# A fused attention and two-MLP kernel: later units with two heads swapped, exponentials with sums on ScalarE, one rectifier, and one block's weights split on chip

## The chip, the cores and the metric

The kernel runs on one core of a Trainium2 chip. The metric is the device time of one execution in microseconds (us), the median over runs. The engines that matter are TensorE (PE, matrix products; PEld are its weight loads), VectorE (DVE), ScalarE (ACT) and SyncE (SP), from whose queue nearly all DMAs are issued. GpSimd (POOL) only sets up constants.

## The reference

q, k and v are [8 batches, 8 heads, 576 positions, 64]. The MLP weights come as 64-bit floats. What is computed:

```python
# attention within chunks of 64 positions
scores = scale * q_c @ k_c.T            # 9 chunks of 64x64 for each batch and head
scores -= max(scores); attn = exp(scores); attn /= sum(attn) + 1e-9
x = attn @ v_c                          # heads side by side: x is [4608, 512]
# first MLP, 2048 hidden features
h = x @ w_in
x = (max(h, 0) + alpha * min(h, 0)) @ w_out
# second MLP, 1536 hidden features
g = x @ w_gate
out = (g * sigmoid(g) * (x @ w_val)) @ w_out2
```

## The kernel before

**Blocks.** The 4608 tokens are nine blocks of 512. Blocks 0 to 7 are the first 512 positions of each batch; block 8, the odd one, is the last 64 positions of all eight batches. Activations stand with features on the partitions and tokens along the free dimension.

**Products.** Each float32 operand is split into two float32r parts, a rounded high one (a copy, on ACT or DVE) and the remainder (a subtraction, DVE). `mm3` (L532) makes one product of three PE instructions of 128x512 columns. Blocks go through an MLP in pairs by a Strassen-like scheme with seven products in place of eight (`operands`, `layer1`, `layer2`). Blocks 0, 1 and 8 of the first MLP and block 0 of the second go singly and plainly (`plain1`, `plain2`): for each of 16 tiles of hidden features, `plain1` takes a weight tile from the function `weights(m)`, does twelve instructions into bank Y0 or Y1 and hands the bank to `outs`. While blocks 0 and 1 go through, the 64-bit weights are converted to float32 (`convert`, `new_tile`), split (`whole`), and stored in DRAM: the split parts of each block of the weight matrix in a `Layer` (`lay_in`, `lay_out`, `lay_b`, `lay_out2`), and the first layer's float32 tile `c` in `cd` (L812). `cs` is a ring of three such tiles, `wring` one of seven split tiles, `hring` (h) one of two.

**Block 8's first layer** (L921) takes `weights = stored(lay_in, ...)` (L678): two loads of 256 KB for each of 16 tiles, each load a split quarter with both of its parts, straight into a tile of `wring`.

**Attention** (L384). A unit is one block and one pair of heads, so there are 36. The heads of a pair, j = 0 and 1, stand on partitions 0 to 63 and 64 to 127. The 16 units of blocks 0 to 3 are `early`: they transpose q and k on PE (L430) through banks X0 and X1 and have the scores in W0 and W1. The 20 later units (blocks 8, 4, 5, 6, 7, started at given products by `heads`, L871) run inside the MLP of other blocks, transpose q and k on DVE, and use banks a0 and a1 alone. For the softmax DVE takes the maximum (L452) and subtracts it (L454) for each head, ACT does one exponential of the whole tile `pp` (L457), DVE sums (L458), inverts (L460) and multiplies (L464). PE transposes the probabilities into a0 (L468), a copy makes `pT`, and the product with v (L472 to L477) goes into a1: for each of eight chunks, head 0 from partitions 0 to 63 to 0 to 63 and head 1 from 64 to 127 to 64 to 127. Each of these float32 products is two PE instructions of 64x64. The result goes through `xo` to x1d in DRAM, or for the first eight units (`direct`) straight into operands.

**The rectifier** (`leaky`, L689): from the sum h (or straight from the bank, where `s` is None) ACT makes max(h, 0) and max(-h, 0) (L705, L706), the second into a tile of `hring`, and DVE joins them with -alpha (L714). Another form, on DVE alone (L710), stands as an alternative and does not appear in the trace.

**The order.** All work is put as items into `Program` with its engine, a cost in us, the items that it depends on, and a latency. `order` (L50) simulates these costs, gives each item a due time that it derives backwards from the chained PE products (`main=True`), and writes out one static order; copies may go to ACT or to DVE, whichever the simulation finds better. Each engine, and SP's queue, then works through its own instructions in that order. Until the first product PE gets filler matmuls (L974).

## Time and profile before

| | |
|---|---|
| median of 3 runs | 1733.77 us (1724.03 to 1735.01) |
| the profiled execution | 1724.21 us, of it 1722.4 from the first to the last instruction |
| PE busy | 1644.0 us (95% of the span) |
| DVE busy | 1232.2 us (72%) |
| ACT busy | 915.0 us (53%) |
| first product of the first layer starts | at 46.67 us |
| block 8's first layer, second layer | from 450.20 us, from 507.30 us |

PE is busy nearly all the time, DVE and ACT are not, and their work lies beside PE's. What one of them does costs time only where PE waits for it. Since queues are static, an instruction that waits holds up all that stands behind it on its engine.

### The profile page before, as it was taken

The page shows a single profiled execution, that of the slowest core. Times are in us where ns is not written, and L with a number is a line of the kernel's source. Part 1 is how long each engine was busy: PE and PEld are TensorE (multiplying, and loading weights), DVE is VectorE, ACT ScalarE, POOL GpSimd, SP SyncE. Part 2 cuts the span into 40 slices and gives each one's busy share as a digit, 9 for nine tenths or more (in the row PEclk, how much of TensorE's full clock was granted, in tenths as well). Part 3 has the DMA queues.
Part 4 walks back from the last instruction along what each step waited for, and adds up shares of the span by engine and source line. Part 5 has one row for each costly group of instructions (what it writes and reads, how often), then busy time and mean ns, then how long its engine had stood idle before and what let it go on. Part 6 is the DMA issues. An engine that isn't in the chain of part 4 may idle for free.

```text
span 1722.4 us, 26328 instructions
## 1 busy us (share of the span) xinstructions
PE 1644.0 (95%) x9260; PEld 1336.3 (78%) x9260; DVE 1232.2 (72%) x2188; ACT 915.0 (53%) x1614; POOL 1.0 (0%) x8
## 2 busy tenths in 40 slices
PE   6999998999989799999999999999999999999998
PEld 5777886778767687877788788778778888788877
DVE  5787886898667689877666964688769534774475
ACT  5777646774453677554444633564576432543352
POOL 0000000000000000000000000000000000000000
PEclk9999999999999899999999999999999999999999
DMA  8978878778999995788755597897855855576555
GB/s 191 264 255 247 291 254 277 236 224 234 247 262 322 324 352 191 264 275 290 273 194 194 187 237 228 215 258 226 258 190 186 283 201 191 190 218 210 195 185 146
DMA packets 350835, 407.57 MB, mean 237 GB/s; under 512 B 208624, under 2 KB 229104, under 8 KB 350704
## 3 DMA queue, kind: packets, MB, share of 16 engines
q1 hardware_dynamic: 348640, 405.89, 75.1%
q8 instruction: 73, 1.20, 0.3%
q14 instruction: 58, 0.48, 0.1%
q10 hardware_dynamic: 2064, 0.01, 0.1%
HBM read 307.24 MB, written 98.57 MB: 236 GB/s over the span
## 4 chain that ended last, share of the span: by engine, by line
PE 52%; DMA 2%; DVE 2%; ACT 1%; issue 0%; DVEq 0%; SPq 0%; ACTq 0%
PE X L533 9%; PE X L534 9%; PE X L535 9%; PE W L533 5%; PE W L535 5%; PE W L534 5%; PE Y L534 2%; PE Y L535 2%; PE Y L533 2%; PE X L672 1%; DMA raw<-in_moe_w_gate_dram 1%; PE W L672 1%; DMA raw<-in_moe_w_val_dram 1%; PE a L476 1%; DVE h L237 0%
## 5 line engine op out<-in xcount | busy, mean ns | idle before, releaser
L533 PE MATMUL X<-op,w 128*128 128x512 f32 x1024 | 407.5, 398 | 22.0 <-DVE h L237 12.3
L534 PE MATMUL X<-op,w 128*128 128x512 f32 x1024 | 401.3, 392 | 0.0
L535 PE MATMUL X<-op,w 128*128 128x512 f32 x1024 | 401.1, 392 | 0.0
L533 PEld LDWEIGHTS X<-op,w 128*128 128x128 f32 x1024 | 193.4, 189 | 75.9 <-ACT s L232 19.1
L232 ACT ACTIVATE op<-g 128x512 fp32r<-128x512 f32 x300 | 182.3, 629 | 125.4 <-PE X L534 44.4
L533 PE MATMUL Y<-op,w 128*128 128x512 f32 x560 | 223.5, 399 | 4.4 <-ACT g L743 2.4
L535 PEld LDWEIGHTS X<-op,w 128*128 128x128 f32 x1024 | 193.6, 189 | 40.8
L534 PEld LDWEIGHTS X<-op,w 128*128 128x128 f32 x1024 | 193.5, 189 | 38.2
L533 PE MATMUL W<-op,w 128*128 128x512 f32 x544 | 213.7, 393 | 9.0 <-ACT h L232 8.9
L534 PE MATMUL Y<-op,w 128*128 128x512 f32 x560 | 219.0, 391 | 1.3 <-DVE w L237 1.3
L535 PE MATMUL Y<-op,w 128*128 128x512 f32 x560 | 218.9, 391 | 0.0
L237 DVE TENSOR_TENSOR op<-g,op 128x512 fp32r<-128x512 f32 x300 | 195.6, 685 | 27.5 <-ACT op L232 22.9
L535 PE MATMUL W<-op,w 128*128 128x512 f32 x544 | 212.3, 390 | 0.0
L534 PE MATMUL W<-op,w 128*128 128x512 f32 x544 | 212.2, 390 | 0.0
L232 ACT ACTIVATE s<-X 128x512 f32<-128x512 f32 x172 | 102.4, 597 | 111.0 <-PE X L535 109.6
L237 DVE TENSOR_TENSOR h<-Y,s 128x512 f32<-128x512 f32 x86 | 58.9, 689 | 142.7 <-PE Y L535 141.7
L533 PEld LDWEIGHTS Y<-op,w 128*128 128x128 f32 x560 | 105.7, 189 | 29.1 <-ACT g L743 2.9
L533 PEld LDWEIGHTS W<-op,w 128*128 128x128 f32 x544 | 102.4, 188 | 31.7 <-ACT h L232 9.7
L534 PEld LDWEIGHTS Y<-op,w 128*128 128x128 f32 x560 | 105.7, 189 | 23.1 <-DVE w L237 2.3
L535 PEld LDWEIGHTS Y<-op,w 128*128 128x128 f32 x560 | 105.5, 188 | 22.5
L535 PEld LDWEIGHTS W<-op,w 128*128 128x128 f32 x544 | 102.4, 188 | 21.4
L534 PEld LDWEIGHTS W<-op,w 128*128 128x128 f32 x544 | 102.5, 188 | 21.0
(146 smaller groups left out, 2096.2 us busy)
## 6 DMA issues: line engine op xcount, KB each, us to landing
w<-l_out SPq DMA_DIRECT2D x168, 512.0 KB, 3.7
w<-l_b SPq DMA_DIRECT2D x126, 512.0 KB, 4.3
w<-l_in SPq DMA_DIRECT2D x56, 512.0 KB, 5.0
l_b<-w SPq DMA_DIRECT2D x84, 256.0 KB, 3.3
l_out<-cw SPq DMA_DIRECT2D x80, 256.0 KB, 4.7
l_in<-w SPq DMA_DIRECT2D x64, 256.0 KB, 4.1
raw<-in_moe_w_out_dram SPq DMA_DIRECT2D x28, 512.0 KB, 5.1
w<-l_in SPq DMA_DIRECT2D x56, 256.0 KB, 4.9
```

Source lines behind the costliest of these rows:

```text
L232: pr.add([("ACT", act(n), lambda: na.activation(out=dst, in_=src, func=AF.Copy), False), ("DVE", dvep(n) if psum else dve1(n), lambda: nv. ...
L237: item("DVE", dve2(n), lambda: nv.tensor_tensor(out=dst, in0=a, in1=b, op=op), reads, writes, **kw)
L476: npe.matmul(out=bank["a1"][rs, ts], lhsT=v4[rs, c, :], rhs=pT[rs, ts], start=True, stop=True)
L533: npe.matmul(out=acc, lhsT=w[:, 0, wk], rhs=x[:, 0, :n], start=first, stop=False, skip_group_check=True)
L534: npe.matmul(out=acc, lhsT=w[:, 1, wk], rhs=x[:, 0, :n], start=False, stop=False, skip_group_check=True)
L535: npe.matmul(out=acc, lhsT=w[:, 0, wk], rhs=x[:, 1, :n], start=False, stop=stop, skip_group_check=True)
L672: npe.matmul(out=acc, lhsT=t[:, gp, a * P:(a + 1) * P], rhs=w[:, :, wp, :], start=first and i == 0, stop=stop and i == 2, skip_group_check ...
```

## The change

- Block 8's first layer gets `weights = split_again`: one load of 256 KB of the float32 tile from `cd` into a tile of `cs`, and a split on chip by `whole` (a copy and a subtraction). The parts that only `stored` read from there (number 21, eight of them) are no longer stored in `lay_in`.
- In all units the subtractions and the sum on DVE go. DVE scales the two maxima by -scale (eight columns); ACT then does eight exponentials of 128x64, for each head's bank one for each pair of chunks, straight from the bank into `pp`, with the scaled maximum as bias and the sum as second output.
- In later units (`turn`) the chunks are numbered so that each transposed tile of `pp` holds, for the second half of the chunks, the heads swapped: head 1 on partitions 0 to 63 and head 0 on 64 to 127. V is loaded to match, in four DMAs instead of two. The product with v then goes from partitions j to partitions j into a1 for the first half and crosswise into a0 for the second, the four kinds in turn. `xo` is copied in two halves.
- The rectifier is h + (1 - alpha) max(-h, 0): one rectification on ACT, one joining step on DVE, which now reads h itself; no tile of `hring` where `s` is None. The cost given to the planner for ACT is halved.

```diff
-    lay_in = Layer("l_in", uses1(qa) + [(x, 21) for x in qa])
+    lay_in = Layer("l_in", uses1(qa))
...
+        turn = not early
...
+                for c0, n, r in ((0, 4, j), (4, 4, 1 - j)) if turn else ((0, NCH, j),):
+                    src = v[i, 2 * hp + j, c0 * CH:(c0 + n) * CH, :].rearrange("(c p) e -> p c e", p=CH) \
+                        if i < B else v[c0:c0 + n, 2 * hp + j, NB:S, :].rearrange("b p e -> p b e")
+                    nsp.dma_start(out=v4[r * 64:(r + 1) * 64, c0:c0 + n], in_=src)
...
+        def chunk(cc, c2):
+            return NCH // 2 * (cc % 2) + cc // 2 * 2 + c2 if turn else 2 * cc + c2
...
-            item("DVE", 0.43, partial(nv.tensor_tensor, out=p4[:, :, j, :], in0=sc[j],
-                                      in1=mx[:, j].to_broadcast([P, NCH // 2, CH]), op=ALU.subtract),
-                 [mk], ["pp", sb_[j]])
-        item("ACT", 0.63, lambda: na.activation(out=pp, in_=pp, func=AF.Exp, scale=scale), [], ["pp"])
-        item("DVE", 0.62, lambda: nv.tensor_reduce(out=sm, in_=p4, axis=AX.X, op=ALU.add), ["pp"], [sk])
+        item("DVE", 0.17, partial(nv.tensor_scalar, out=mx, in0=mx, scalar1=-scale, scalar2=None, op0=ALU.mult),
+             [], [mk])
+        def exps(j):
+            for cc in range(NCH // 2):
+                h = j ^ (turn and cc % 2)
+                na.activation(out=p4[:, cc, h, :], in_=sc[j][:, cc, :], func=AF.Exp, scale=scale, bias=mx[:, j, cc],
+                              accum_out=sm[:, cc, h])
+        for j in range(2):
+            item("ACT", 0.96, partial(exps, j), [mk], ["pp", sk, sb_[j]])
...
-            for c in range(NCH):
-                for j in range(2):
-                    rs, ts = slice(64 * j, 64 * j + 64), slice(CH * c, CH * c + CH)
-                    npe.matmul(out=bank["a1"][rs, ts], lhsT=v4[rs, c, :], rhs=pT[rs, ts], start=True, stop=True)
-        item("PE", 1.2, pv, ["pT", kv], ["a1"])
+            for x in range(NCH // 2):
+                for y, j in ((0, 0), (0, 1), (1, 0), (1, 1)):
+                    cc, c2, r = 2 * (x // 2) + y, x % 2, j ^ (turn and y)
+                    c, rs = chunk(cc, c2), slice(64 * r, 64 * r + 64)
+                    npe.matmul(out=bank["a0" if turn and y else "a1"][64 * j:64 * j + 64, CH * c:CH * c + CH],
+                               lhsT=v4[rs, c, :], rhs=pT[rs, (2 * cc + c2) * CH:(2 * cc + c2 + 1) * CH],
+                               start=True, stop=True)
+        pb = ["a1", "a0"] if turn else ["a1"]
+        item("PE", 0.75 if turn else 1.2, pv, ["pT", kv], pb)
...
-        copy_(xo, bank["a1"], NB, [], [xk, "a1"])
+        for y, b in enumerate(pb):
+            h = slice(y * G, (y + 1) * G) if turn else slice(0, NB)
+            copy_(xo[:, h], bank[b][:, h], NB // len(pb), [], [xk, b])
...
-        def relus():
-            how["relu"] = True
-            na.activation(out=g, in_=src, func=AF.Relu)
-            na.activation(out=h, in_=src, func=AF.Relu, scale=-1.0)
+        def minus():
+            how["minus"] = True
+            na.activation(out=g, in_=src, func=AF.Relu, scale=-1.0)
...
-                nv.scalar_tensor_tensor(out=g, in0=h, scalar=nal, in1=g, op0=ALU.mult, op1=ALU.add)
+                nv.scalar_tensor_tensor(out=g, in0=g, scalar=rest, in1=src, op0=ALU.mult, op1=ALU.add)
...
-        pr.add([("ACT", 2 * act(n), relus, False),
-                ("DVE", dvep(n) if psum else dve1(n), lows, not psum)], rd, [gk, tk, *wr])
+        pr.add([("ACT", act(n), minus, False),
+                ("DVE", dvep(n) if psum else dve1(n), lows, not psum)], rd, [gk, *wr])
...
+    def split_again(m):
+        c, ck = cs.next()
+        dma(NB * 4 * P, lambda: nsp.dma_start(out=c, in_=cd[m]), [("cd", m)], [ck])
+        return whole(c, ck)
...
-        plain1(qa, [(x, 0)], partial(stored, lay_in, IN, a_), leak)
+        plain1(qa, [(x, 0)], split_again, leak)
```

## Rows read from the trace of the kernel before

**Rows 1.** The head of the page: span, and busy time of each engine.
```profile
span 1722.4 us, 26328 instructions
PE 1644.0 (95%) x9260; PEld 1336.3 (78%) x9260; DVE 1232.2 (72%) x2188; ACT 915.0 (53%) x1614; POOL 1.0 (0%) x8
```

**Rows 2.** Busy time by stretch: start:end, length, then engines, clock, DMA share, GB/s.
```profile
0.00:47.00 47.00, 31.03 (x462) 26.97 (x463) 24.15 (x55) 26.01 (x35) 0.98 (x8) 0.93 0.83 189
47.00:180.00 133.00, 125.65 (x1176) 101.18 (x1175) 110.00 (x220) 95.61 (x167) 0.00 (x0) 0.99 0.86 260
430.00:490.00 60.00, 55.27 (x414) 44.01 (x413) 41.60 (x79) 27.73 (x52) 0.00 (x0) 1.00 0.96 240
490.00:565.00 75.00, 67.30 (x485) 53.70 (x483) 50.44 (x105) 32.21 (x65) 0.00 (x0) 0.98 0.99 307
1060.00:1200.00 140.00, 138.07 (x1058) 110.58 (x1057) 101.35 (x186) 74.24 (x118) 0.00 (x0) 1.00 0.80 226
```

**Rows 3.** PE's waits, 430 to 600 us: for whom, us in total, times, longest.
```profile
PE W L533 <- ACT h L232: 7.6, 1, 7.6
PE a L468 <- DVE pp L237: 6.8, 4, 3.6
PE a L476 <- ACT pT L232: 4.3, 2, 2.4
PE Y L533 <- ACT h L706: 1.2, 1, 1.2
```

**Rows 4.** PE's timeline around one V product and one group of scores: start, length.
```profile
355.09 1.15 PE L476 MATMUL a<-pT,v 64*64 64x64 f32 x32 [0.69 <-ACT pT L232]
356.17 0.50 PE L533 MATMUL X<-op,w 128*128 128x512 f32 x1
...
364.55 0.69 PE L445 MATMUL a<-kT,qT 64*64 64x64 f32 x32
365.18 0.50 PE L533 MATMUL W<-op,w 128*128 128x512 f32 x1
```

**Rows 5.** The same two, instructions in flight in their first 0.1 us.
```profile
355.09 0.27 PE L476 MATMUL a<-pT,v 64*64 64x64 f32 x2 [0.69 <-ACT pT L232]
...
364.55 0.29 PE L445 MATMUL a<-kT,qT 64*64 64x64 f32 x4
```

**Rows 6.** Groups by line and shape: count, busy us, mean ns; ACT reading banks.
```profile
L232 ACT ACTIVATE s<-W 128x512 f32<-128x512 f32 x86 | 50.9, 593 | 85.2 <-PE W L535 84.6
...
L232 ACT ACTIVATE c<-W 128x256 f32<-128x256 f32 x4 | 1.3, 382 | 3.4 <-DMA out_dram<-c 2.2 <-PE W L672 1.3
```

**Rows 7.** The same view: the softmax steps that go, and a split's subtraction.
```profile
L458 DVE TENSOR_REDUCE sm<-pp 128x8 f32<-128x512 f32 x36 | 24.4, 677 | 19.3 <-ACT pp L457 18.7
L457 ACT ACTIVATE pp<-pp 128x512 f32<-128x512 f32 x36 | 22.8, 632 | 27.5 <-DVE pp L977 27.5
...
L237 DVE TENSOR_TENSOR w<-c,w 128x512 fp32r<-128x512 f32 x32 | 22.0, 687 | 8.5 <-ACT w L232 8.5
...
L977 DVE TENSOR_TENSOR pp<-a,mx 128x256 f32<-128x256 f32 x40 | 17.0, 424 | 1.3
```

**Rows 8.** Busy time by stretch of line 706, the second rectifier, alone.
```profile
47.00:180.00 133.00, 19.15 (x32) 0.99 0.86 260
```

**Rows 9.** PE's waits, 0 to 200 us: the longest in total.
```profile
PE X L430 <- DMA qk<-in_k_dram: 10.2, 9, 2.0
```

**Rows 10.** ACT's timeline in block 8's first layer.
```profile
457.97 0.60 ACT L706 ACTIVATE h<-Y 128x512 f32<-128x512 f32 x1 [3.26 <-DMA x2d<-h]
458.47 0.59 ACT L705 ACTIVATE g<-Y 128x512 f32<-128x512 f32 x1
```

**Rows 11.** DMA issues, 430 to 490 us: count, size, median us to landing.
```profile
w<-l_in SPq DMA_DIRECT2D x32, 256.0 KB, 5.5
```

**Rows 12.** Groups by line and shape: ACT's strided copy of transposed q.
```profile
L232 ACT ACTIVATE qT<-X 128x512 f32<-128x512 f32 x16 | 17.6, 1102 | 8.6 <-PE X L430 8.1 <-PE W L445 0.3
```

More of the change, by code (lines that the diff above doesn't have):

```diff
@@ L195, in attention_moe_moe2 @@
     alpha_sb = one("alpha_sb", [P, KF])
-    nalpha_sb = one("nalpha_sb", [P, KF])
-    zero = one("zero", [P, KF])
+    rest_sb = one("rest_sb", [P, KF])
+    ones = one("ones", [P, KF])
     ops = Ring(sb, "op", 14, [P, 2, NB], F32R)
@@ L417, in load_v @@
             for j in range(2):
-                src = v[i, 2 * hp + j, 0:NB, :].rearrange("(c p) e -> p c e", p=CH) if i < B else \
-                    v[:, 2 * hp + j, NB:S, :].rearrange("b p e -> p b e")
-                nsp.dma_start(out=v4[j * 64:(j + 1) * 64], in_=src)
+                for c0, n, r in ((0, 4, j), (4, 4, 1 - j)) if turn else ((0, NCH, j),):
+                    src = v[i, 2 * hp + j, c0 * CH:(c0 + n) * CH, :].rearrange("(c p) e -> p c e", p=CH) \
+                        if i < B else v[c0:c0 + n, 2 * hp + j, NB:S, :].rearrange("b p e -> p b e")
+                    nsp.dma_start(out=v4[r * 64:(r + 1) * 64, c0:c0 + n], in_=src)
         item("SP", 0.9 if early else 1.9, lambda: load(tq, q), [], [kq], lat=2.2, **gate)
@@ L442, in scores @@
                 for j, c2 in ((0, 0), (1, 1), (0, 1), (1, 0)):
-                    c = 2 * cc + c2
+                    c = chunk(cc, c2)
                     rs, ts = slice(64 * j, 64 * j + 64), slice(CH * c, CH * c + CH)
@@ L692, in leaky @@
         g, gk = gts[j][c][:, :n], ("g", j, c)
-        t, tk = hring.next()
-        h = t[:, :n]
         if s is not None:
-            add2(h, acc, s[0], ALU.add, n, [s[1]], [tk, b], psum=True)
-            src, rd, wr = h, [tk], []
+            t, tk = hring.next()
+            src = t[:, :n]
+            add2(src, acc, s[0], ALU.add, n, [s[1]], [tk, b], psum=True)
+            rd, wr = [tk], []
         else:
             src, rd, wr = acc, [], [b]
-        al, nal = alpha_sb[:, m:m + 1], nalpha_sb[:, m:m + 1]
+        al, rest = alpha_sb[:, m:m + 1], rest_sb[:, m:m + 1]
         how = {}
-        def relus():
-            how["relu"] = True
-            na.activation(out=g, in_=src, func=AF.Relu)
-            na.activation(out=h, in_=src, func=AF.Relu, scale=-1.0)
+        def minus():
+            how["minus"] = True
+            na.activation(out=g, in_=src, func=AF.Relu, scale=-1.0)
         def lows():
-            how["relu"] = False
+            how["minus"] = False
             nv.tensor_scalar(out=g, in0=src, scalar1=0.0, scalar2=al, op0=ALU.min, op1=ALU.mult)
         def join():
-            if how["relu"]:
-                nv.scalar_tensor_tensor(out=g, in0=h, scalar=nal, in1=g, op0=ALU.mult, op1=ALU.add)
+            if how["minus"]:
+                nv.scalar_tensor_tensor(out=g, in0=g, scalar=rest, in1=src, op0=ALU.mult, op1=ALU.add)
             else:
@@ L717, in leaky @@
         psum = s is None
-        pr.add([("ACT", 2 * act(n), relus, False),
-                ("DVE", dvep(n) if psum else dve1(n), lows, not psum)], rd, [gk, tk, *wr])
-        item("DVE", dve2(n), join, rd, [gk, tk, *wr], port=not psum)
+        pr.add([("ACT", act(n), minus, False),
+                ("DVE", dvep(n) if psum else dve1(n), lows, not psum)], rd, [gk, *wr])
+        item("DVE", dve2(n), join, rd, [gk, *wr], port=not psum)
     def to_x2(m, c, acc, b, s, n, pair):
@@ L847, in attention_moe_moe2 @@
         make_identity(nc, ident)
-        ng.memset(zero, 0.0)
+        ng.memset(ones, 1.0)
         na.dma_start(out=alpha_sb, in_=alpha.rearrange("(m p) -> p m", p=P))
-        ng.tensor_tensor(out=nalpha_sb, in0=zero, in1=alpha_sb, op=ALU.subtract)
+        ng.tensor_tensor(out=rest_sb, in0=ones, in1=alpha_sb, op=ALU.subtract)
         leak = partial(leaky, n=NB)
```

## The prediction

> **What bounds the kernel now.** I read the head of the page first: a span of 1722.4 us in a profiled execution of 1724.2, with TensorE (PE) busy 95% of it [rows 1]. Next comes the busy time by stretch [rows 2]. Between 1060 and 1200 us, where eight attention units run inside another layer, PE is busy 138.07 of 140 us. There a microsecond of PE work is a microsecond of time, and one of VectorE (DVE) or ScalarE (ACT) is not. The stretches that differ are the start (PE busy 31.03 of 47 us, part of that filler) and the odd block, block 8: 55.27 of 60 and 67.30 of 75 us, with the DMA share at 0.96 and 0.99 against 0.80 elsewhere. The last view for this is what PE waited for from 430 to 600 us [rows 3]: 6.8 us in four waits for DVE's normalised probabilities, 4.3 us in two for ACT's copy pT, 1.2 us for a rectifier and 7.6 us, once, for ACT's eviction of block 8. So the kernel is PE-bound, with holes in block 8 and at the start that come from late chains. The first kind of saving is PE work anywhere; the second is whatever makes those chains earlier.
>
> **The change part by part.**
>
> *Heads swapped in later units.* Now the product with V takes 32 instructions on two quarters of PE, from 355.09 to the next product at 356.17: 1.08 us. The scores, also 32 instructions of 64x64, use all four quarters and take 364.55 to 365.18: 0.63 us [rows 4]. The first moments tell why: 2 instructions of the former are in flight just after its start, and 4 of the latter [rows 5]. After the change the later units' V product visits the four quarters in turn, as the scores do, so I price it at the scores' 0.63: 0.45 us saved in each of the 36 - 16 = 20 later units, 9.0 us in all. The bounds are 0 and 9.0. Nothing hides this, for it is PE time; only a unit that stands in a hole already may lose it to the wait behind. The probabilities' transposes and the scores keep their number. V's load becomes four issues instead of two with the same bytes; x1's copy becomes two halves, 0.38 + 0.38 us against 0.59 [rows 6], both behind the product, and the plan sets the store 12 us ahead of need.
>
> A rule speaks against this part. In the trace, the V product of before has both of its instructions in flight at once, and these two read partitions 0 to 63 and 64 to 127 and write one bank, a1 [rows 5]. The Trainium skill, "TensorEngine Tiling (Array Packing)", Restrictions and Gotchas, says that different row tiles cannot access the same PSUM bank simultaneously. By that rule the swapped product, which still puts two row tiles into each of a0 and a1, would not reach the scores' rate and its term would be 0 instead of 9.0; the trace disagrees, since the two did run together.
>
> *Exponentials with sums on ScalarE.* DVE loses two subtractions of 0.42 and a sum of 0.68 and gains a tiny scaling, about 0.2: 1.3 us less per unit, 47 us over 36 units. ACT loses one exponential of 0.63 and gains eight of 128x64, each with a bias per partition and a sum [rows 7]. No row shows such an instruction. From ACT's reads of PSUM, 593 ns for 512 columns and 382 for 256 [rows 6], 64 columns extrapolate to 382 - 192 x 0.824 = 224 ns. That is the lower bound (1.8 us a unit), and 382 the upper (3.1). I take 0.30, above the lower because bias and sum come on top: 2.4 us, 1.8 more than now per unit. The skill's page "ScalarE: Activation LUTs", What ACT_TABLE_LOAD costs, gives 280 ns + 0.833 ns a column with a pointer bias and 93 ns of overlap, from which I estimate 240 ns in a row; by it a unit's extra would be 1.3 us instead of 1.8, and no run here shows it yet.
>
> On the path this matters where something waits. The softmax chain itself hardly moves: DVE is 1.3 shorter, ACT 1.8 longer. But four exponentials now stand together on ACT (1.2 us), and copies that free a bank queue behind them. Between 1060 and 1200 us I allow 2 us of new PE waits for that, against the 2 us of holes there now. At the start I allow 2 more: ACT is busy 26.01 of 47 us, so five units' extra (9 us) fits, and from 47 to 180 us the remaining eleven add 20 to 95.61 of 133 while the rectifier takes off 16 (below) [rows 2, 8]. PE's waits at the start are mostly for loads of q and k (10.2 us for k alone, nine waits [rows 9]), which the change leaves alone. Four microseconds together; bounds 0 and 36 (16 early units x (8 x 0.36 - 0.63) if fully exposed).
>
> *One rectifier.* ACT's second rectification goes: about 0.5 us from start to start [rows 10], 32 times before 180 us [rows 8]. DVE's joining step keeps its length but now reads its input itself, so the bank of a direct product stays taken until DVE is through. The buffer h is not used by direct products any more: at 457.97 the second rectifier waited 3.26 us for an earlier store of h [rows 10], and PE 1.2 us for it [rows 3]. That wait goes: 1.2 us. Otherwise ACT is not the bound, so the rest is counted at nothing; if DVE were late with the join, PE would wait for the bank.
>
> *Block 8's first layer from float32 tiles.* Its 32 loads of 256 KB between 430 and 490 us [rows 11] become 16, so 4.2 MB and 16 issues go. At the 307 GB/s of the next stretch [rows 2] that is 13.7 us of transfer out of a stretch whose queues are full. Eight stores of 256 KB at the start go too, at a share of 0.86: counted at nothing. In exchange come 16 splits, 0.63 on ACT (a copy like L457's 632 ns) and 0.69 on DVE [rows 7], which lie beside PE work: DVE goes from 41.60 of 60 to about 41.6 + 11 - 5 = 48, ACT has more room. With three buffers the loads run at most three tiles ahead; the conversions of later weights need the same buffers and queue behind them, but these are not needed for 200 us. If the cover failed, each split would cost PE 1.3 us, 21 in all. What the relief buys: the six waits for attention (6.8 + 4.3 = 11.1 us) end in chains that begin with loads of q, k and v in these same queues. Bounds 0 and 11.1; I take half, 5.5. The 7.6 us of the eviction wait for stores through two buffers and stay.
>
> Sum: 1724.2 - 9.0 - 1.2 - 5.5 + 4 = 1712.5, so 1712. This goes by the profiled execution; the median of the runs shown, 1733.8, is 0.6% above it, the lowest run (1724.0) equals it. I forecast on the profile's scale and let the range take the scatter.
>
> **Rivals.**
> 1. More of the holes close. If the DMA relief takes all 11.1 us and half of the 7.6: 1724.2 - 9.0 - 1.2 - 11.1 - 3.8 + 0 = 1699. For it: shares of 0.96 and 0.99. Against it: the second half of block 8 keeps its own loads, and one of its waits is 3.6 us.
> 2. The splits come late. The stage trades loads that needed no engine for a chain load, ACT, DVE, with a prefetch of three; half of the 21 us exposed gives 1712.5 + 10.5 = 1723, no change. Against it: DVE is free 30% of this stretch.
> 3. The V product gets no faster (the bank rule, or the quarters collide): 1724.2 - 1.2 - 5.5 + 4 = 1721.5. Against it: both patterns run already, in the V product and in the scores.
> 4. Slower: ScalarE becomes the bound at the start, where PE has nothing else to do and each unit's chain crosses ACT five times. It outweighs the rest, beyond measurement, once all of 16 early units expose over 2.6 us each: 1724.2 - 9.0 - 1.2 + 16 x 2.43 (at 0.382 us each) = 1753. For it: ACT's two strided copies already take 1.1 us each there [rows 12]. Against it: ACT is idle for 21 of the first 47 us, and PE's waits name loads.
>
> **How the numbers follow.** The likeliest case, 0.48, has 1712 and its own range 1703 to 1721. Rival 1 has 0.15, rival 2 0.17, rival 3 0.08, rival 4 0.12. One per cent of the median, about what a measurement tells from no change, puts the limits at 1716.4 and 1751.1. Faster: three quarters of the likeliest case (0.36), all of rival 1 (0.15), a little of the others (0.02): 0.53. Slower: some 0.07, the upper part of rival 4. The same: 0.40. The range 1696 to 1740 leaves out the lowest part of rival 1 and most of rival 4.
>
> **What would show it.** In the profile after, 32 V instructions of a later unit should take 0.63 us to the next product (1.08 would be rival 3). Eight exponentials of a unit should take 2.0 to 2.8 us of ACT; DVE should be some 36 us less busy (47 less, 11 more) and ACT some 12 less (36 x 1.8 + 16 x 0.63 more, and 144 rectifiers of 0.60 fewer: 16 tiles of hidden features by nine blocks). Loads of float32 tiles should number 16 between 430 and 490 us, with the DMA share there below 0.9 and PE's waits for pT and the probabilities in block 8 halved. Waits of PE for the split weights would be rival 2. First products that start clearly after 47 us with ACT over 90% busy before them would be rival 4. The forecast is wrong if the order, made by a planner that knows none of these true lengths, puts new waits where I looked for none.

## The result and the profile after

The median went from 1730.87 us (4 runs of the kernel before on the same chip, 1724.03 to 1735.01) to 1711.32 us (4 runs, 1705.54 to 1712.76). The ratio is 0.9881, with a 95% interval of 0.986 to 0.9902. The profiled execution of the changed kernel took 1712.76 us with a span of 1711.0; that of the kernel before had a span of 1722.4 [rows 1], so the two traces that can be compared line by line are 11.4 us apart. The medians are 19.6 us apart: the profiled execution of before (1724.2) is at the short end of its runs, and that of after (1712.76) is the longest of its four. The traces therefore explain 11 of the 20 us; the rest has no trace.

The head of the page after (span, busy time of each engine), to be held against [rows 1]:

```profile
span 1711.0 us, 26853 instructions
PE 1637.5 (96%) x9256; PEld 1332.2 (78%) x9256; DVE 1196.6 (70%) x2130; ACT 911.3 (53%) x2048; POOL 1.0 (0%) x8
```

DVE lost 35.6 us, as worked out. PE lost 6.5 us of busy time and about 5 us of idle time.

Busy time by stretch, after (start:end, length, engines, clock, DMA share, GB/s), the same stretches as [rows 2]:

```profile
0.00:47.00 47.00, 33.87 (x463) 28.90 (x464) 21.37 (x52) 34.69 (x111) 0.97 (x8) 0.96 0.86 194
47.00:180.00 133.00, 122.96 (x1157) 99.89 (x1156) 96.18 (x195) 98.39 (x301) 0.00 (x0) 0.96 0.82 245
430.00:490.00 60.00, 57.48 (x425) 45.66 (x424) 42.98 (x79) 39.72 (x118) 0.00 (x0) 0.97 0.81 213
490.00:565.00 75.00, 64.48 (x480) 50.95 (x478) 49.96 (x106) 35.88 (x109) 0.00 (x0) 0.97 0.91 297
1060.00:1200.00 140.00, 135.03 (x1059) 106.69 (x1058) 99.47 (x182) 90.19 (x251) 0.00 (x0) 1.00 0.83 229
```

Two things are to be seen. In block 8's first layer the DMA share fell from 0.96 to 0.81 and PE was busy for 2.2 us more of the 60 us. Between 1060 and 1200 us, where a PE microsecond is a microsecond of time, PE is now idle for 5.0 us instead of 1.9: what the V product gave there, something else took.

Windows at fixed times drift apart between two kernels. The table below cuts each trace at its own instructions instead. Every version computes its large products with the same 6480 PE instructions (three for each product of 128x128 by 128x512). A column is the time from the start of one of them to the start of another, counted in the order in which they start. In the kernel after the cuts lie at 311.5, 449.6, 555.7, 754.1, 1012.3, 1197.5, 1228.2 and 1703.2 us. Block 8 falls into the third column, and the eight units of rows 1060 to 1200 into the sixth.

```
               0-907  -1425  -1814  -2592  -3564  -4276 -4406 -6473
before         309.0  137.8  116.1  196.7  260.1  185.1  34.1  475.7
after          311.5  138.1  106.2  198.4  258.2  185.1  30.7  475.1
e1_pairs       312.1  139.3  111.7  199.5  258.5  187.4  30.4  475.1
e8_double      309.9  138.8  118.4  199.9  258.9  185.2  30.4  475.0
e2_stored      311.4  139.2  119.8  194.9  262.2  186.7  30.6  475.1
e3_softmax     308.1  153.8  111.0  193.8  262.3  182.0  32.9  475.1
e4_two_relus   314.0  141.1  110.0  194.4  260.7  185.1  30.7  475.7
b_swap         312.4  139.0  118.9  196.9  258.6  182.1  34.5  475.6
b_split        310.3  144.0  107.9  200.2  260.4  185.1  34.2  475.6
b_exp          310.9  146.9  118.0  198.4  259.3  189.6  30.4  475.6
b_rect         307.8  145.0  116.9  195.7  260.1  185.1  32.6  475.1
e7_cost        310.6  138.8  108.0  199.5  258.2  185.7  30.4  475.1
e6_evict       312.2  141.4  109.5  186.5  259.5  185.1  30.6  475.1
e9_both        306.6  141.2  109.1  186.7  261.3  185.2  30.4  475.0
```

After minus before, column by column: +2.5, +0.3, -9.9, +1.7, -1.9, 0.0, -3.4, -0.6. That sums to -11.3, the spans' 11.4. By the columns, nearly all of the profiled gain is in block 8 (-9.9) and in a wait that I had not looked at (-3.4). But a column is not one part of the change. Each column is one execution: the first holds the same instructions in the same order in after, e1_pairs and e8_double, and reads 311.5, 312.1 and 309.9 us, so a difference of 2 us there tells nothing.

Block 8's column taken apart, before and then after: the busy time of its stretch, the same for the V product's line alone, and PE's waits in it:

```profile
446.80:562.90 116.10, 105.61 (x767) 84.19 (x766) 76.50 (x154) 52.55 (x103) 0.00 (x0) 0.99 0.97 278
446.80:562.90 116.10, 6.89 (x192) 6.07 (x192) 0.99 0.97 278
PE a L468 <- DVE pp L237: 6.8, 4, 3.6
PE a L476 <- ACT pT L232: 2.4, 1, 2.4
PE Y L533 <- ACT h L706: 1.2, 1, 1.2
...
449.60:555.70 106.10, 102.41 (x766) 81.72 (x765) 75.03 (x152) 61.65 (x189) 0.00 (x0) 0.98 0.87 263
449.60:555.70 106.10, 4.31 (x192) 3.44 (x192) 0.98 0.87 263
PE a L490 <- ACT pT L232: 3.0, 1, 3.0
PE a L481 <- DVE pp L237: 0.7, 1, 0.7
```

PE's idle time there fell from 10.5 to 3.7 us: the waits for the probabilities and pT from 9.2 to 3.7 (-5.5), the rectifier's wait from 1.2 to nothing. Another 2.6 us are V products, six of which lie in this column; the remaining 0.6 is other PE work. The V product's line fell by 2.3 us in the second column too (6.89 to 4.61) and by 3.6 in the sixth (9.18 to 5.56), 8.5 in all. Those two columns did not get shorter, because PE's idle time grew by 1.8 us in the second (2.9 to 4.7) and by 3.0 in the sixth (1.9 to 5.0).

PE's waits of after from 430 to 600 us (for whom, us, times, longest; compare [rows 3]):

```profile
PE W L552 <- ACT h L232: 8.6, 1, 8.6
PE a L481 <- DVE pp L237: 3.2, 2, 2.5
PE a L490 <- ACT pT L232: 3.0, 1, 3.0
PE X L552 <- ACT s L232: 2.0, 2, 1.3
```

The waits for probabilities and for pT went from 11.1 to 6.2 us. The eviction wait stayed and got 1.0 longer. The wait of [rows 3] for a rectifier is gone, and the waits for copies of another product have gone from 0.7 us (one wait) to 2.0 (two).

### The profile page after: what moved, and what is told of

The parts are those of the page before. It is cut to its first block, busy times and chain, and to the rows that moved or that the text cites. A ratio compares the mean times of both kernels' runs of the same rounds, so it can differ in the third digit from the quotient of the medians.

```text
span 1711.0 us, 26853 instructions
## 1 busy us (share of the span) xinstructions
PE 1637.5 (96%) x9256; PEld 1332.2 (78%) x9256; DVE 1196.6 (70%) x2130; ACT 911.3 (53%) x2048; POOL 1.0 (0%) x8
## 4 chain that ended last, share of the span: by engine, by line
PE 82%; DMA 8%; ACT 4%; DVE 3%; SPq 1%; issue 1%; ACTq 0%; DVEq 0%
PE X L552 13%; PE X L553 12%; PE X L554 12%; PE Y L552 6%; PE Y L553 6%; PE Y L554 6%; PE W L552 6%; PE W L553 6%; PE W L554 6%; DMA qk<-in_q_dram 2%; PE a L490 1%; ACT pp L468 1%; DMA x2d<-h 1%; PE X L691 1%; DMA raw<-in_moe_w_val_dram 1%
## 5 line engine op out<-in xcount | busy, mean ns | idle before, releaser
L232 ACT ACTIVATE s<-X 128x512 f32<-128x512 f32 x172 | 102.4, 599 | 119.5 <-PE X L554 118.4
L552 PEld LDWEIGHTS W<-op,w 128*128 128x128 f32 x544 | 102.7, 189 | 32.9 <-ACT h L232 10.7
```

What stands on the lines that cost most here:

```text
L232: pr.add([("ACT", act(n), lambda: na.activation(out=dst, in_=src, func=AF.Copy), False), ("DVE", dvep(n) if psum else dve1(n), lambda: nv. ...
L552: npe.matmul(out=acc, lhsT=w[:, 0, wk], rhs=x[:, 0, :n], start=first, stop=False, skip_group_check=True)
```

## The experiments

Some of the kernels below differ from their parent in the order in which the planner puts work on the engines, not in the edited work alone, because each edit changes the items that it plans. Only two, e1_pairs and e8_double, keep the order of PE, DVE and ACT of the kernel after exactly; that is why they carry most of the argument. The experiments ran on two chips, on which the kernel before took 1734.84 us (e1 to e4) and 1730.0 to 1730.75 us (the others), so a ratio to it compares better than microseconds do.

**e1_pairs: the V product without its interleaving.** The same 32 instructions, the straight quarters first and then the crosswise ones; the plan does not see it.

```diff
-            for x in range(NCH // 2):
-                for y, j in ((0, 0), (0, 1), (1, 0), (1, 1)):
+            steps = [(x, y, j) for x in range(NCH // 2) for y, j in ((0, 0), (0, 1), (1, 0), (1, 1))]
+            if turn:
+                steps.sort(key=lambda z: z[1])
+            for x, y, j in steps:
```

> The changed kernel with one thing altered: in later units the V product visits its eight crosswise quarters after its eight straight ones, so that two quarters of PE work at a time as in the kernel before. Plan, loads, copies and the order on every queue stay those of the changed kernel. Theory (PE is the bound, so its work counts in full): the product takes 1.08 us again, and 20 x 0.45 = 9.0 us come back: span about 1720 against 1711 of the changed kernel, ratio to the kernel before about 0.993 against 0.988. Rival (the saving falls into waits that follow): the product takes 1.08 us and the span stays within 3 us of 1711.

PE's timeline, first of the kernel after, with what is in flight in the first 0.05 us of the product behind it, as in [rows 4, 5]:

```profile
1089.32 0.69 PE L490 MATMUL a<-pT,v 64*64 64x64 f32 x32
1089.94 0.50 PE L552 MATMUL X<-op,w 128*128 128x512 f32 x1
...
1089.32 0.29 PE L490 MATMUL a<-pT,v 64*64 64x64 f32 x4
```

and then of e1_pairs:

```profile
1098.22 0.98 PE L492 MATMUL a<-pT,v 64*64 64x64 f32 x32
1099.13 0.50 PE L554 MATMUL X<-op,w 128*128 128x512 f32 x1
```

The swapped product takes 0.62 us to the next product with four instructions in flight, and 0.91 us sorted into pairs. I had expected the 1.08 of [rows 4] for the sorted one; at the change from straight to crosswise quarters, four run together for a moment. So e1_pairs takes back 0.29 x 20 = 5.8 us of PE work, and not the whole 9. It measured 1720.60 us, a ratio of 0.9925 to before [0.9908, 0.9942], against 0.9881: 9.3 us by the medians, 7.6 by the ratios, and 10.7 by the profiled spans. In the sixth column, without holes, it costs 2.3 us, and eight units by 0.29 are 2.3: there a PE microsecond is a microsecond. In block 8 it costs 5.5, more than the six units there can owe by themselves (1.7 us): PE also stands idle for 2.2 us longer there, and why isn't shown.

**e8_double: the traffic of block 8 put back.** Every float32 tile is loaded twice, the second time into a tile that is free and that nobody reads: 16 issues more on SP's queue, the same order on all other engines. One more thing moves: the first three tiles are loaded at 422 to 437 us instead of 319 to 323, since each load is issued together with its copy, whose tile is not free earlier. The first two splits are no later for it (437.1 and 439.2 us, in after 437.9 and 439.8).

```diff
+        e, ek = gkey(m // 2, 1 + 2 * (m % 2))
+        def both():
+            nsp.dma_start(out=c, in_=cd[m])
+            nsp.dma_start(out=e, in_=cd[m])
-        dma(NB * 4 * P, lambda: nsp.dma_start(out=c, in_=cd[m]), [("cd", m)], [ck])
+        dma(NB * 4 * P, both, [("cd", m)], [ck, ek])
```

> The changed kernel with 16 more loads of 256 KB in block 8's first layer: each float32 tile is loaded a second time into a tile that nothing reads then. The plan and the order on PE, DVE and ACT are those of the changed kernel; only SP's queue has 16 more issues. So the traffic and the number of loads are those of the stored parts again, but no product depends on the second load. Theory (the 16 us that undoing the split cost, between 447 and 517 us, are traffic and queue time, which delay q, k and v): 6 to 12 us longer than the changed kernel, 1717 to 1723, lost in block 8, with the DMA share of 430 to 490 us back near 0.95. Rival (the products' own wait for two loads each, or the plan made from their cost, lost them): within 3 us of 1711.

It measured 1725.42 us, 0.9964 [0.9948, 0.998], more than the 6 to 12 us expected: 14.1 us of the gain gone, by the ratios too (0.83% of 1731 is 14.4). The profiled span is 13.5 longer, and 12.2 of it is block 8's column (118.4 against 106.2). Busy time by stretch of e8_double, and then ACT's longest wait of 430 to 510 us and PE's waits of 430 to 570:

```profile
430.00:490.00 60.00, 51.58 (x386) 39.84 (x385) 34.27 (x62) 31.24 (x87) 0.00 (x0) 0.94 0.93 252
...
ACT w L232 <- DMA c<-cd: 15.0, 8, 4.3
...
PE a L490 <- ACT pT L232: 5.4, 3, 4.1
PE Y L552 <- DVE g L733: 4.2, 3, 2.4
PE a L481 <- DVE pp L237: 4.2, 4, 2.0
```

With the share at 0.93 instead of 0.81, PE does 5.9 us less in these 60 us. ACT waits 15.0 us for the tiles that it is to split; in the kernel after that row does not exist. PE's waits for pT and the probabilities are back at 9.6 us, near the 11.1 of before, and its clock stands at 0.94. So it is the transfers and their place in SP's queue that cost, and not what the engines do in block 8. The price is not that of the kernel before, though, which has no split: ACT's wait for tiles can't occur there, and how much of the 12.2 us it makes isn't shown.

**e2_stored and b_split: the same part undone, and done alone.**

```diff
-    lay_in = Layer("l_in", uses1(qa))
+    lay_in = Layer("l_in", uses1(qa) + [(x, 21) for x in qa])
...
-        plain1(qa, [(x, 0)], split_again, leak)
+        plain1(qa, [(x, 0)], partial(stored, lay_in, IN, a_), leak)
```

> The changed kernel with block 8's first layer as before: 32 loads of 256 KB of stored parts, no split on chip, and eight more stores at the start. Theory (the DMA queues were the late link of block 8): PE's waits for pT and the probabilities between 430 and 565 us go from 6 back to about 11, the DMA share of 430 to 490 us goes from 0.81 to about 0.95, and the span is about 5 us longer, 1716. Rival (the planner's new order, not the relief, closed the holes): share back at 0.95, span within 2 us of 1711.

> The kernel before with only block 8's first layer changed: float32 tiles loaded and split on chip. Theory (the split's gain stands by itself): 8 to 12 us shorter than the kernel before, span about 1714, ratio about 0.994, gained between 447 and 527 us. Rival (it gains only together with the shorter V product and the lighter DVE): 3 us or less.

Undone: 1727.99 us, 0.9967 [0.9953, 0.9982], 16.7 above after by the medians and 14.9 by the ratios, where 5 were expected. Done alone (the same lines in reverse, on the kernel before): 1723.77 us, 0.9961 [0.9945, 0.9977], 7 us below before, a little less than the 8 to 12 expected. Read the table's third column from top to bottom: every version with the split and single loads is at 106.2 to 111.7 us, every one without it (before, e2_stored, b_swap, b_exp, b_rect) at 116.1 to 119.8, and e8_double, which has the split and the traffic, at 118.4. Only the seventh parts the versions as cleanly, by the softmax. Alone, the split takes 8.2 us off its column (116.1 to 107.9), which is more than the 5.5 us of waits between before and after and less than the 12.2 and 13.6 that the two undoings cost there.

DMA issues of the kernel after, 430 to 490 us (count, size, median us to landing):

```profile
c<-cd SPq DMA_DIRECT2D x13, 256.0 KB, 3.3
qk<-in_q_dram SPq DMA_DIRECT2D x16, 64.0 KB, 3.1
```

and of the kernel before:

```profile
qk<-in_q_dram SPq DMA_DIRECT2D x12, 64.0 KB, 5.4
```

Against the 32 loads of [rows 11] there are 13 (the other three, as many as there are buffers, came earlier), each landing in 3.3 us instead of 5.5, and q lands in 3.1 us instead of 5.4. In e8_double, with the engines' order of after, q is back at 5.3 us. The loads of q are where the chain begins that ends in the probabilities.

**e3_softmax and b_exp: the old softmax in the kernel after; the new one alone in before.**

```diff
-        item("DVE", 0.17, partial(nv.tensor_scalar, out=mx, in0=mx, scalar1=-scale, scalar2=None, op0=ALU.mult),
-             [], [mk])
...
-            item("ACT", 0.96, partial(exps, j), [mk], ["pp", sk, sb_[j]])
...
+            item("DVE", 0.43, partial(nv.tensor_tensor, out=dst, in0=src, in1=top, op=ALU.subtract),
+                 [mk], ["pp", sb_[j]])
+        item("ACT", 0.63, lambda: na.activation(out=pp, in_=pp, func=AF.Exp, scale=scale), [], ["pp"])
+        item("DVE", 0.62, lambda: nv.tensor_reduce(out=sm, in_=p4, axis=AX.X, op=ALU.add), ["pp"], [sk])
```

> The changed kernel with the old softmax: two subtractions on DVE, one exponential of the whole tile, the sum on DVE; swapped heads, split and rectifier stay. Theory (the eight exponentials, 2.46 us together, cost PE about 4 us, 2 at the start and 2 between 1060 and 1200 us, and the relief of DVE is worth nothing as DVE is not the bound): the span is about 4 us shorter, 1707, with fewer waits of PE for the probabilities between 1060 and 1200 us. Rival (DVE's 1.3 us a unit is on the path, at the start above all): 5 us or more longer, with the first product back at 46 to 47 us from 43.87.

> The kernel before with only the new softmax: eight exponentials with sums on ACT in all units. Theory (DVE's relief is worth something only where the other parts fill DVE, the splits in block 8; alone it brings an earlier first product and loses it again before 180 us): within 5 us of 1722.4. Rival (what undoing it cost, 16 us, is its own): 10 us or more shorter.

Both miss what was expected (4 us shorter; within 5 us), and the two answers look contradictory: without the new softmax the final kernel is slower (1727.48 us, 0.9956 [0.9942, 0.9971]), and with it alone the old kernel is slower too (1736.80 us, 1.0036 [1.0019, 1.0053]). The columns tell them apart. In the sixth, the new softmax costs 3.1 us (after against e3_softmax: 185.1 and 182.0) to 4.5 us (b_exp against before: 189.6 and 185.1), both times. In the first column it costs 3.4 (after against e3_softmax) or 1.9 us (b_exp against before), hardly more than the 2.2 by which that column differs where nothing in it does. In the seventh it gains: 30.4 to 30.7 with it, 32.6 to 34.5 without, in all fourteen versions. What makes e3_softmax slow is the second column, 153.8 us against 138.1, where PE has one long wait (PE's timeline):

```profile
322.10 0.80 PE L552 MATMUL X<-op,w 128*128 128x512 f32 x1 [5.87 <-DVE h L237]
```

Busy time from 300 to 350 us in e3_softmax and, second, in after:

```profile
300.00:350.00 50.00, 44.13 (x183) 36.00 (x182) 35.68 (x68) 23.44 (x45) 0.00 (x0) 0.93 0.76 231
...
300.00:350.00 50.00, 47.98 (x239) 38.84 (x239) 39.86 (x73) 27.34 (x53) 0.00 (x0) 1.00 0.77 237
```

DVE, which the old softmax loads more, is busy for less of this stretch in e3_softmax (35.68 us) than in after (39.86). So PE's wait for DVE isn't an overloaded DVE. DVE's timeline of e3_softmax, and then SP's queue, show what it was:

```profile
319.76 0.42 DVE L237 TENSOR_TENSOR t<-c 128x256 f32<-128x256 f32 x1 [8.21 <-DMA c<-cd]
...
321.36 0.68 DVE L237 TENSOR_TENSOR h<-X,s 128x512 f32<-128x512 f32 x1
...
302.88 6.46 SPq L413 DMA_DIRECT2D qk<-in_q_dram  x8
309.88 3.92 SPq L413 DMA_DIRECT2D qk<-in_k_dram  x8
315.33 0.43 SPq L847 DMA_DIRECT2D c<-cd  x1
```

DVE stood still for 8.21 us for a float32 weight tile whose load SP issued at 315.33 us at the earliest, behind the sixteen issues of a unit's q and k; the addition that empties PE's bank X came after that in DVE's order. In after the longest wait of this kind in the stretch is 3.9 us. So this wait comes from the order on SP's queue and not from the old softmax's work. Of the column's 15.7 us it is 5.9, PE's other waits there are 5.1 longer than in after, and the rest is PE's busy time: behind the wait its granted clock is 0.51 from 322 to 328 us. In b_rect it is the same: DVE waits 7.4 us for such a tile, and PE 5.0 us for the addition behind it.

What the exponentials themselves do is plain. ACT's timeline of one later unit in the kernel after, and what PE waits for behind it:

```profile
1098.80 1.28 ACT L468 ACT_TABLE_LOAD   x1 [0.30 <-DVE mx L1002]
1100.10 0.31 ACT L468 ACTIVATE pp<-a,mx 128x64 f32<-128x64 f32 x1
1100.31 0.19 ACT L468 ACTIVATION_READ_ACCUMULATOR pp<-a,mx 128x1 f32 x1
1100.40 0.30 ACT L468 ACTIVATE pp<-a,mx 128x64 f32<-128x64 f32 x1
...
1102.13 0.35 ACT L468 ACTIVATE pp<-a,mx 128x64 f32<-128x64 f32 x1
1102.33 0.24 ACT L468 ACTIVATION_READ_ACCUMULATOR pp<-a,mx 128x1 f32 x1
1102.42 0.64 ACT L232 ACTIVATE s<-X 128x512 f32<-128x512 f32 x1
...
1103.11 0.50 PE L552 MATMUL X<-op,w 128*128 128x512 f32 x1 [1.14 <-ACT s L232]
```

Each exponential is followed by an instruction of its own that reads the sum out. From start to start a pair is 0.30 us, and the eight take 2.3 us until the next copy starts. That copy `s<-X` frees a bank; it stands behind the eight, and PE waits 1.14 us for it: the place that the prediction named.

**e4_two_relus and b_rect: the old rectifier in after; the new one alone in before.**

```diff
-            na.activation(out=g, in_=src, func=AF.Relu, scale=-1.0)
+            na.activation(out=g, in_=src, func=AF.Relu)
+            na.activation(out=h, in_=src, func=AF.Relu, scale=-1.0)
...
-                nv.scalar_tensor_tensor(out=g, in0=g, scalar=rest, in1=src, op0=ALU.mult, op1=ALU.add)
+                nv.scalar_tensor_tensor(out=g, in0=h, scalar=nal, in1=g, op0=ALU.mult, op1=ALU.add)
```

> The changed kernel with the old rectifier: two rectifications on ACT, the second into a tile of h. Theory (ACT is not the bound; only the wait behind a store of h was on the path): 1 to 3 us longer, 1712 to 1714, with ACT's busy time up by about 80 us. Rival (the room that the rectifier makes on ACT is what pays for the exponentials, 16 us of it before 180 us): 8 us or more longer, most of it before 310 us.

> The kernel before with only the one-rectifier form. Theory (ACT is not the bound; the wait behind a store of h goes): 1 to 4 us shorter than 1722.4. Rival (what undoing it cost, 8.6 us, is its own): 7 us or more shorter.

Undone: 1721.73 us, 0.9933 [0.9918, 0.9947], longer by more than the 8 us that the rival asked for, though not before 310 us. Alone: 1731.84 us, 1.0016 [1.0, 1.0032], not shorter. Undone, the differences to after are spread over five columns (+2.5, +3.0, +3.8, -4.0, +2.5); alone, the second column loses 7.2 us and the others give some of it back. Both kernels have an order of their own, and the size of this part can't be read from them. What the trace of after does show is the new wait that was possible: PE for the joining step on DVE, which now holds the bank. PE's waits from 0 to 200 us, the longest and the new one:

```profile
PE X L432 <- DMA qk<-in_q_dram: 10.3, 6, 4.7
PE Y L552 <- DVE g L733: 1.8, 1, 1.8
```

The same row stands at 4.2 us in three waits in e8_double's block 8 (above), where DVE is late.

**b_swap: the swapped heads alone.** The chunks, the four loads of V, the interleaved product and the halves of `xo` from the change's diff, on the kernel before, with the old softmax writing to the new places.

```diff
+        turn = not early
...
+                for c0, n, r in ((0, 4, j), (4, 4, 1 - j)) if turn else ((0, NCH, j),):
...
+                for y, j in ((0, 0), (0, 1), (1, 0), (1, 1)):
...
+        pb = ["a1", "a0"] if turn else ["a1"]
```

> The kernel before with only the swapped heads of the later units (softmax on DVE as before, written to the swapped places). Theory (PE work counts in full wherever PE is the bound): 20 x 0.45 = 9.0 us shorter, less what falls into the holes of block 8: span 1715 to 1718 against 1722.4, ratio about 0.996. Rival (the gain needs the other parts): 3 us or less.

1729.96 us, 0.9996 [0.9978, 1.0013]: no gain, where 0.996 was expected. Yet the sixth column is 182.1 us against 185.1, and eight units by 0.45 are 3.6. The time is lost elsewhere: +3.4 in the first column and +2.8 in block 8, where the order is another one.

**e7_cost: the planner told of ACT's true length.** It plans each half of a unit's exponentials at 0.96 us, and the trace has about 1.2.

```diff
-            item("ACT", 0.96, partial(exps, j), [mk], ["pp", sk, sb_[j]])
+            item("ACT", 1.23, partial(exps, j), [mk], ["pp", sk, sb_[j]])
```

> The changed kernel with nothing altered but the planner's cost of each half of the exponentials, 1.23 us as measured in place of 0.96. Theory (the plan's error makes PE's waits for the probabilities and for pT, 16 us in all): 2 to 5 us shorter than 1711. Rival (waits come from late loads, and a plan with another cost is only another order): within 3 us either way, or longer; if it is longer by 5 us or more, an order drawn anew costs that much by itself, and the single undoings hold that much that isn't theirs.

1713.95 us, 0.9902 [0.9878, 0.9926], not below after (0.9881 [0.986, 0.9902]). The waits that the exponentials cause don't come from the plan's error: with the true length the sixth column is 185.7 instead of 185.1.

**e6_evict: the remaining eviction wait.** Block 8's four results leave through four tiles that are free at that time, instead of two that wait for earlier stores.

```diff
             for f, b in enumerate(banks):
+                if i == 8:
+                    t, tk = gkey(JA - 1 - f // 2, 1 + 2 * (f % 2))
+                    copy_(t, bank[b], NB, [], [tk, b])
+                    dma(NB * 4 * P, partial(lambda t, f: nsp.dma_start(out=x2d[:, 2 * (f // 2) + f % 2, i * NB:(i + 1) * NB],
+                                                                       in_=t), t, f), [tk], [("x2", i, 2 * (f // 2) + f % 2)])
+                    continue
                 to_x2(f % 2, 2 * (f // 2), bank[b], b, None, NB, (i,))
```

> The changed kernel with block 8's second layer's results copied into four separate free tiles instead of through the two of h. Theory (PE's wait of 8.6 us at 567 us is ACT's third copy waiting for a store from one of two buffers): the wait shrinks to 1 to 3 us, 5 to 8 us shorter than 1711, 1703 to 1706. Rival (the operands of the next layer are late at the same place anyway, and the wait goes over to them): 2 us or less.

The timelines around it, in after (ACT, then two of PE) and in e6_evict:

```profile
566.08 1.22 ACT L232 ACTIVATE h<-W 128x512 f32<-128x512 f32 x2 [2.23 <-DMA x2d<-h]
...
566.73 0.80 PE L552 MATMUL W<-op,w 128*128 128x512 f32 x1 [8.56 <-ACT h L232]
567.33 0.63 PE L553 MATMUL W<-op,w 128*128 128x512 f32 x1
```

```profile
566.66 0.50 PE L552 MATMUL W<-op,w 128*128 128x512 f32 x1 [1.13 <-ACT turned L232]
```

The wait went from 8.56 to 1.13 us. The fourth column shrank by 11.9 us, more than the 7.4. Another wait in it, for ACT's g, is 2.1 us shorter, and PE's busy time there fell by 2.0 us, from 182.92 to 180.92, for in after PE comes out of the long wait at the lower of its two clock levels (granted 0.50 from 566 to 570 us; the second line takes 0.63 us, where 0.39 is usual). But the new order costs 3.3 us in each of the second and third columns, and the median is 1704.99 us, 0.9847 [0.9821, 0.9874]: 6.3 us below after.

**e9_both: e6_evict, and the swap in eight of the early units too** (those whose result goes through x1d in DRAM).

```diff
-        turn = not early
+        turn = not direct
```

> A version beyond both: the changed kernel with block 8's results evicted through four free tiles, and with the heads swapped in the eight early units that go through DRAM as well. Theory: against the version with the eviction alone (span 1707.6) 8 x 0.45 = 3.6 us of PE work go, and PE is busy from 100 to 180 us but for a few holes: 2 to 4 us shorter, 1704 to 1706, ratio about 0.983. Rival (there PE waits for the next q anyway, and the doubled issues of v make that later): no shorter than 1707.6.

1703.55 us, 0.9848 [0.9824, 0.9871]: the same as e6_evict within what can be measured. The first column is 5.6 us shorter than in e6_evict, more than 8 x 0.45, and 1.8 of it is given back in the fifth. This is the fastest version of the study, with e6_evict beside it.

**Whether the parts add.** Alone, the four parts change the ratio by -0.0004 (swap), -0.0039 (split), +0.0036 (exponentials) and +0.0016 (rectifier), together +0.0009; all at once they give -0.0119. Undone one by one (the swap only by its 0.29 of 0.46), they cost 0.0044, 0.0086, 0.0075 and 0.0052, together 0.0257. Neither sum is near the change's 0.0119. The second column shows most of the reason: the parts have little to do there (six V products, which took 6.89 us in before), yet it ranges from 137.8 us (before) to 153.8 (e3_softmax), and before and after happen to have two of the best orders in it. The four parts on the kernel before lose 1.2, 6.2, 9.1 and 7.2 us there. So each number of a kernel planned anew holds its part plus an order drawn anew. Two orders have the four parts and nothing else, after (0.9881) and e7_cost (0.9902), so the gain does not hang on one of them alone; e6_evict and e9_both are lower, but their fourth column gains some 12 us by the tiles that e6_evict adds.

## Why the prediction was right, and where it was not

The forecast was 1712 us; the profiled execution took 1712.76, and the median is 1711.32. The sum was made on the profile's scale, and there most of its terms were met. That the median met the number too is partly luck: 11.7 us off the median of before, 1730.87, would have been 1719, and the medians differ by 19.6.

*PE is the bound, with holes in block 8 and at the start.* This held. Where PE is busy without a hole, the 0.29 us a unit of e1_pairs came out as 2.3 us for eight units. In block 8 most of the time came from waits, 6.8 of 9.9 us.

*V product, -9.0 us.* Its price was right: 0.62 us, 0.63 forecast. The traces have 8.5 us less of it in the later units, 2.3, 2.6 and 3.6 in the second, third and sixth columns. The objection from the Trainium skill, "TensorEngine Tiling (Array Packing)", Restrictions and Gotchas (different row tiles can't access one PSUM bank at a time), does not hold for this case: the two row tiles both write a0 and both write a1, each to its own half of the partitions, four instructions are in flight, and the rate is that of the scores. Rival 3 is out. What the whole kernel owes to it is only bounded: e1_pairs takes back 5.8 us of PE work and costs 7.6 to 10.7, while the swap alone, with its own order, gained nothing.

*Exponentials, +4 us.* The length was right: 0.30 us each. The estimate from the Trainium skill, "ScalarE: Activation LUTs", What ACT_TABLE_LOAD costs, was 0.24 and is too low here; the trace has a second instruction behind each that reads the sum. The term for 1060 to 1200 us was too small: PE's idle time in the sixth column grew by 3.0 us, and the two pairs of kernels give 3.1 and 4.5, instead of 2. This is why after and before have the same 185.1 us in that column: the exponentials ate the V product's 3.6. The start has 2.5 us more in its column (2 allowed), hardly beyond that column's scatter, and not as waits: PE's idle time there is 31.0 us before and 30.6 after, and between 47 and 180 us its granted clock is 0.96 instead of 0.99. The upper bound of 36 us was worked out with 0.36 us an exponential, below the 0.382 named as the highest price; with that it is 39. Not foreseen at all was the seventh column's -3.4: in before PE stood still for 1.82 us at 1223 us, at the head of the next layer, and came back at the lower clock level (granted 0.57 from 1223 to 1227 us). Every version with the new softmax is without that wait; what PE waited for there isn't shown.

PE's timeline of before at that place:

```profile
1223.16 0.52 PE L533 MATMUL X<-op,w 128*128 128x512 f32 x1 [1.82 <-issue]
1223.47 0.63 PE L534 MATMUL X<-op,w 128*128 128x512 f32 x1
```

*Rival 4, ScalarE the bound at the start.* Out: ACT is busy 34.69 of the first 47 us (26.01 + 9 = 35 was worked out), the first large product starts at 43.87 us, before at 46.67, and PE's longest wait there is still for loads. b_exp is 0.36% slower than before, but it loses 9.1 us in the second column and 4.5 in the sixth, and only 1.9 in the first. The rival's own sum left out block 8's -5.5; with it, 1753 would have been 1747, and the 2.6 us a unit that it needed lies above its highest price of 2.43.

*Rectifier, -1.2 us.* The wait went, as said, and another came: 1.8 us for DVE's join, which had been counted at nothing with the condition that DVE is in time. Its net size stays open.

*Block 8, -5.5 us.* The mechanism was right (float32 loads instead of stored parts, the share between 430 and 490 us below 0.9, no wait of PE for the split weights, so rival 2 is out), and so was the size: the waits for pT and the probabilities are 5.5 us shorter in block 8's column, 4.9 from 430 to 600 us. The column's 9.9 us are not this term alone, since 2.6 of them are V products and 1.2 the rectifier's wait. But the choice of half of 11.1 us rested on no row, so the exact hit is luck. And the part has no single price: alone it took 8.2 us off this column, and undoing it cost 12.2 (e8_double) and 13.6 (e2_stored). In those two PE's clock from 430 to 490 us is 0.94, against 0.97 in after, and e8_double shows a wait that I had not counted, ACT for the loads themselves (15.0 us), which makes everything behind it in ACT's order late. Rival 1 asked for all of the 11.1 us and half of the eviction wait; 4.9 of the 11.1 went, and the eviction wait grew.

*The eviction wait stays.* Right: 8.56 us. e6_evict shows what it was worth: 11.9 us in its column, of which 7.4 are the wait itself.

*ACT and DVE.* DVE's -36 came out as -35.6. ACT's -12 came out as -3.7. The exponentials' line added 67.5 us (96.70 against 29.17) instead of 64.8, and the halves of x1's copy, which were not in that sum, add 1.4. The second rectifiers' line had 88.48 us, but they overlap their neighbours, 0.5 us from start to start [rows 10] for 0.60 each, so their going frees less of ACT's busy time than the 86 us that the sum took off.

*What stays open.* The size of the rectifier's part; what PE waited for at 1223 us in before; why the waits of the second column changed; and how much of e8_double's loss is ACT's wait for tiles.

So the sum came out because the V product, the rectifier's wait and block 8's waits were met within half a microsecond each, while the rest cancelled: the exponentials cost 5.5 instead of 4, PE's idle time in the second column grew by 1.8, and against both stands the seventh column's 3.4. That cancelling is luck.

## What to carry to other kernels

When a column of time gets shorter, take it apart before giving it to one part of a change: the waits that went, the work that went, and the clock. When a stage's transfers fill its queues, a test that doubles the loads and leaves the engines' order as it is shows that the transfers cost time; what it costs also holds what the new kernel alone would wait for. Where a planner draws the order anew with each edit, parts undone or done alone do not add up to the whole; cut the traces at the same instructions and compare columns, trust most the edits that leave the order alone, and read a late engine's own waits before calling it overloaded. An engine's microsecond that moves to one with room is free only until a bank's copy stands behind it.

## What the runs showed of the hardware

An exponential with a sum is two instructions on ACT, an ACTIVATE and an ACTIVATION_READ_ACCUMULATOR of 0.19 to 0.24 us that overlaps it; the pair takes 0.30 us from start to start for 64 columns. Four 64x64 quarters of PE ran at once into two banks, with two row tiles in each bank. With that they took 0.62 us for 32 instructions, the rate of the scores (0.63), whose row tiles write different banks. And in the same stretch of the program, loads of q of 64 KB landed in 5.4 us at a DMA share of 0.96 (before), in 5.3 at 0.93 (e8_double) and in 3.1 us at 0.81 (after).
